# Reordering experts by size in a routed two-layer network, with the weight splits of short steps moved

## The chip, the cores and the metric

The kernel runs on one core of a Trainium2 chip. The metric is the time of one execution on the device in microseconds (us); the median of three runs of the kernel before is 1150.44 us. The trace is one profiled execution. Engines are named as in the profile: PE (TensorE, matmuls), PEld (its weight loads), DVE (VectorE), ACT (ScalarE), POOL (GpSimd) and SP (SyncE); the last two also issue transfers (DMAs).

## The reference

Three parts follow one another: a cross attention, a gated network without routing, and a network with eight experts, of which each row uses the one that wins an argmax. Only the last is touched here.

```python
def _moe2_ref(x, w_gate, w_output_gate, w1, w2):      # x: 4352 x 512
    logits = x @ w_gate
    e_idx = np.argmax(logits, axis=1)                 # one of 8 experts per row
    ...
    for e in range(E):
        mask = e_idx == e
        if not mask.any():
            continue
        h = np.maximum(x[mask] @ w1[e], 0.0)          # w1[e]: 512 x 1024
        ye = h @ w2[e]                                # w2[e]: 1024 x 512
        out[mask] = gate_w[mask, None] * eom[mask, e, None] * ye
    return out
```

With the inputs used, the reference sends 1082, 32, 576, 64, 512, 1024, 512 and 550 rows to experts 0 to 7.

## The kernel before

The first phase (attention, dense network, routing) runs to about 720 us. It writes every row into a table in device memory, sorted by expert (`ysort`), and counts the rows of each expert. The second phase is the class `Phase2`. It takes the rows expert by expert, in steps: a full step has 256 rows; what is left of an expert at its end, if it is at most 64 rows, is a step of 64 rows ("half" in the code). Which expert comes when is data: `table()` computes on DVE a rank for each expert (`rk`, by its count; the two that were largest when the first weights were fetched are forced to the front), turns it into a one-hot matrix `oh` by comparing `rk` with an iota `rr` (L1303), and from that a table with one line for each step. Each engine reads its fields into registers: `first` and `last` (this is the first, or last, step of its expert, and another expert follows), `slot`, `rank`, `half`, the experts whose weights are to be loaded (`exp2`, `exp1`) and the row to start from. Two full steps of the largest expert run ahead of that loop, with fixed addresses. What the loop then runs is, in the order before (F a full step, h one of 64 rows):

    expert  0    5     2    7    4   6   3  1
    steps   FFh  FFFF  FFh  FFh  FF  FF  h  h      steps 0 to 18

All products are done in two parts: an operand is split into a high part (ACT, a copy that rounds) and a low part (DVE, the difference), and three of the four products are summed. So the weights of each expert are loaded raw and split on ACT and DVE: w1 in four parts (`part1`, L1713 and L1769), w2 in two halves of two parts (`part2`, L1731 and L1777). There are two raw buffers for w1 (`raw1`), one raw buffer for w2 (`raw2`), one split w1 and two slots of split w2. The rules for an expert of rank r are:

- In its first step, ACT and DVE split w2 of rank r+1. When DVE has done the last part (semaphore `l21`), SP loads w2 of rank r+2 into `raw2` (L1028, one transfer of 2 MB).
- In its last step, ACT and DVE split w1 of rank r+1, each part once PE no longer needs the old one. When the last part is done (`l13`), SP loads w1 of rank r+3 (L1031, four transfers of 512 KB).

SP runs through the steps in order, and so do its transfers. An expert with one single step does both in that step.

PE's order in a full step k (L1648, L1655): `p1(k,0)`, then `p2(k-1,3)`, the last quarter of the step before (after a short step: its whole second product `n2(k-1)`), then `p1(k,1)`, `p2(k,0)`, `p1(k,2)`, `p2(k,1)`, `p1(k,3)`, `p2(k,2)`. `p1(k,j)` is a quarter of the first product (24 matmuls), `p2(k,j)` a quarter of the second (12). In a short step it is `n1(k)` (16 matmuls), `p2(k-1,3)`, and `join(k)`, which transposes and folds (16); `n2(k)` (16) follows in the next step. `p2(k,j)` waits for ACT (`hh`, L1098) and DVE (`hl`, L1104) to have split quarter j of the hidden layer; `p1(k,0)` waits for DVE's `yl(k)`, which makes the low part of the step's rows.

ACT and DVE each run a fixed list for a step (L1735 to 1759 and L1862 to 1891). They run it in order: an instruction that waits holds up all behind it. For the short step they are:

    ACT: copy 0, w1(0), copy 1, w1(1), yh(k+1), hhb 0, hhb 1, w1(2), w1(3), w2(0), w2(1)
    DVE: turn(k+1), seen 0, w1(0), seen 1, w1(1), yl(k+1), osc(k-1), hlb 0, hlb 1, w1(2), w1(3), w2(0) to w2(3)

For a full step ACT has hh(0), w2(0), w1(0), hh(1), ..., and DVE hl(0), osc(k-1), w1(0), w2(0), hl(1), turn(k+1), .... An entry w1 or w2 does something only in a last or first step. ACT's `w2(0)` (`hi2`, L1725) waits for the raw w2 to have landed (semaphore `r2`). `osc(k)` scales the finished rows of step k by their gates, in two halves of 128 rows (`gate`, L1114) or, for 64 rows, in two dependent operations (L1839, L1841); POOL then stores them and fetches the rows of step k+2. At the end, `guard.run(step, end)` calls `tail` (PE) and `osc` (DVE) for the last step, which ends with its store.

Of the kernel before, what the change touches and what calls it, by code (L numbers as in the profile page):

```python
# [14 lines left out]
ALU = mybir.AluOpType  # L15
AX = mybir.AxisListType
# [11 lines left out]
NE = 8  # L28
# [918 lines left out]
class Phase2:  # L947
# [207 lines left out]
            return self.w2[:, slot, hl, 512 * c : 512 * c + 512]  # L1155
        return self.w2[:, ds(slot, 1), hl, 512 * c : 512 * c + 512].rearrange("p a f -> p (a f)")

    def p2(self, e, k, j, slot):

        for t in range(2):  # L1160
            i = 0
            for f in range(2):
                for hh, wh in ((0, 0), (0, 1), (1, 0)):
                    m = e.matmul(  # L1164
                        out=self.ps_o[2 * (k % 2) + t],
                        lhsT=self.hT[:, j % 2, f, hh, P * t : P * t + P],
                        rhs=self.w2c(slot, wh, 2 * j + f),
                        start=j == 0 and i == 0,
                        stop=j == 3 and i == 5,
                    )  # L1170
                    i += 1
        return m

    def parts(self):
# [53 lines left out]
    def table(self, cp):  # L1228

        nc = self.nc  # L1230
        V = nc.vector
# [18 lines left out]
        e8, tie = self.e8, self.tie  # L1250
        kk = iota([1], [[0, 1]], cm=1)
        rr = iota([NE, NE], [[1, NE], [0, NE]])
        lt = t([NE, NE])
        nc.gpsimd.memset(lt, 1.0)
        nc.gpsimd.affine_select(
# [4 lines left out]
        nc.tensor.matmul(out=ps[:, 0:NE], lhsT=self.ph.ones, rhs=self.ph.cum, start=True, stop=True)  # L1260
        cnt = t([NE])
        V.tensor_copy(out=cnt, in_=ps[:, 0:NE])

        self.pad = cp.tile([P, NE + 1], I32, name="pad")
        pad = t([NE + 1])
# [34 lines left out]
        )  # L1300
        red(rk, cmp)
        oh = t([NE, NE])
        V.tensor_tensor(out=oh, in0=rk.unsqueeze(1).to_broadcast(sq), in1=rr, op=ALU.is_equal)  # L1303

        def pick(v):
# [11 lines left out]
        m = t([NE, NE])  # L1317
# [16 lines left out]
        def total(o, v, scalar, op0, u=None):  # L1334
# [53 lines left out]
            out=own,  # L1388
# [11 lines left out]

    def run(self):
        tc, nc = self.tc, self.nc
        names = "p q a d yh yl tn o os0 so r10 r11 r2".split()
        names += [f"l1{j}" for j in range(4)] + [f"h1{j}" for j in range(4)]
        names += [f"l2{p}" for p in range(2)] + [f"h2{p}{c}" for p in range(2) for c in range(2)]
        self.s = {n: tc.alloc_semaphore("m_" + n) for n in names}
        self.sy = [tc.alloc_semaphore(f"m_y{i}") for i in range(3)]
        bank = lambda n: self.ph.ps_x.tile([P, 512], F32, tag="aux", name=n)
        self.ps_t = [bank(f"ps_t{i}") for i in range(2)]

        class Guard:
            def __init__(g, eng):
                g.eng = eng
                g.total = None
                g.sure = SURE

            def __call__(g, k, body):
                if k < g.sure:
                    body()
                elif k < NSTEP:  # L1420
                    g.get()
                    with g.eng.If(g.total > k):
                        body()

            def get(g):
                if g.total is None:
                    g.total = g.eng.value_load(self.ttab[0:1, 0:1], min_val=0, max_val=NSTEP)

            def run(g, body, end):

                for i in range(SURE - 1):
                    body(i)
                g.get()

                def rest(i):
                    g.sure = i + 1
                    body(i)
                    if i + 1 == NSTEP:
                        end(i)
                        return  # L1440
                    with g.eng.If(g.total > i + 1):
                        rest(i + 1)
                    with g.eng.Else():
                        g.sure = i + 1
                        end(i)

                rest(SURE - 1)

        with tc.tile_critical(), nc.Block(no_gpsimd_drain=True) as block:
            block.sync(lambda e: self.sp(Guard(nc.sync)))  # L1450
            block.gpsimd(lambda e: self.pool(Guard(nc.gpsimd)))
            block.tensor(lambda e: self.pe(Guard(nc.tensor)))
            block.scalar(lambda e: self.act(Guard(nc.scalar)))
            block.vector(lambda e: self.dve(Guard(nc.vector)))
# [106 lines left out]
    def pe(self, guard):  # L1561
# [34 lines left out]
                after[17] = inc("p")  # L1596
            self.p1(e, j, before, after)

        def p2(k, j):
            thr = [(f"l2{j // 2}", R[k][0])] if k >= 0 else []  # L1600
            o = [("o", 2 * k)] if j == 0 else []
            wait(("d", 6 * k + j + 1 if k >= 0 else 0), *o, *thr)()
            self.p2(e, k, j, R[k][1] if k >= 0 else 0).then_inc(s["q"], 1)

        def product(out, ts, first=True, last=True):
            for i, (l, w) in enumerate(ts):
# [52 lines left out]
            tail(k - 1)  # L1659
            kinds(k, lambda: rest(k), lambda: join(k))  # L1660

        guard.run(step, tail)

    def weights(self, e, k, one, two):

# [12 lines left out]
    def act(self, guard):  # L1678
        e, s = self.nc.scalar, self.s

        def hh(k, j):
            e.wait_ge(s["p"], 5 * k + j + 1 + (j == 3))
            if k + j:
                e.wait_ge(s["q"], self.q2(k, j - 2))
            self.hhi(e, j).then_inc(s["a"], 1)

        def copy(k, n):
            e.wait_ge(s["p"], 5 * k + 2 + n)
            e.activation(out=self.hs[:, 512 * n : 512 * n + 512], in_=self.ps_h[n], func=AF.Copy).then_inc(s["a"], 1)

        def hhb(k, b):
            e.wait_ge(s["p"], 5 * k + 4 + b)
            if k + b:
                e.wait_ge(s["q"], self.q2(k, b - 2))
            e.activation(
                out=self.hTB[:, 4 * b : 4 * b + 4, 0, 0:HB],
                in_=self.ps_t[b].rearrange("p (c n) -> p c n", c=4)[:, :, 0:HB],
                func=AF.Relu,
            ).then_inc(s["a"], 1)

        def yh(k, free):

            e.wait_ge(s["tn"], k)
            for i, f in enumerate(free):
                e.wait_ge(s["p"], 5 * (k - 1) + f)
                self.yhi(e, 2 * i).then_inc(s["yh"], 1)

        def step(k):
            (kind,) = self.load(e, k, "half")

            def hi1(j, slot, rank1, rank, free):
                e.wait_ge(s["p"], 5 * k + free)
                go = lambda x: e.activation(  # L1713
                    out=self.part1(self.w1[:, 0], j), in_=self.part1(self.raw1[:, x], j), func=AF.Copy
                ).then_inc(s[f"h1{j}"], 1)
                with e.If(slot == 0):
                    if j == 0:
                        e.wait_ge(s["r10"], rank1 * 32)
                    go(0)
                with e.Else():  # L1720
                    if j == 0:
                        e.wait_ge(s["r11"], rank1 * 32 + 32)
                    go(1)

            def hi2(p, slot, rank):  # L1725
                if p == 0:
                    e.wait_ge(s["r2"], rank * 16)
                if k + p:
                    e.wait_ge(s["q"], self.q2(k - 1, 2 + p))
                for c in range(2):  # L1730
                    e.activation(  # L1731
                        out=self.w2part(slot, 0, p, c), in_=self.part2(self.raw2, p, c), func=AF.Copy
                    ).then_inc(s[f"h2{p}{c}"], 1)

            w1, w2 = self.weights(e, k, hi1, hi2)  # L1735
            with e.If(kind == 0):
                hh(k, 0)
                w2(0)
                w1(0, 1)
                hh(k, 1)  # L1740
                w2(1)
                w1(1, 2)
                hh(k, 2)
                w1(2, 3)
                guard(k + 1, lambda: yh(k + 1, (4, 5)))
                hh(k, 3)
                w1(3, 5)
            with e.Else():
                copy(k, 0)
                w1(0, 2)  # L1750
                copy(k, 1)
                w1(1, 2)
                guard(k + 1, lambda: yh(k + 1, (3, 3)))
                hhb(k, 0)
                hhb(k, 1)
                w1(2, 3)
                w1(3, 3)
                w2(0)
                w2(1)

        guard.run(step, lambda k: None)

    def dve(self, guard):
# [58 lines left out]
            with e.Else():  # L1822
                go(True)

        def osc(k):
            e.wait_ge(s["q"], self.q2(k, 3))
            if k >= 0:
                e.wait_ge(s["so"], 32 * (k + 1))

            def both():  # L1830
                if k >= 0:
                    e.sem_inc(s["os0"], 1)
                for t in range(2):
                    self.gate(e, k, t).then_inc(s["o"], 1)

            def half():
                ps = self.ps_o[2 * (k % 2)]
                o, g = self.ob[0][0:HB], self.gt[k % 4][0:HB, 0, 0:1]
                e.tensor_scalar(out=o, in0=ps[HB:P], scalar1=g, scalar2=None, op0=ALU.mult).then_inc(s["os0"], 1)  # L1839
# [19 lines left out]
        def step(k):  # L1859
# [17 lines left out]
                w2(3)  # L1877
            with e.Else():
                guard(k + 1, lambda: turn(k + 1))
                seen(k, 0)  # L1880
                w1(0)
                seen(k, 1)
# [4 lines left out]
                hlb(k, 1)  # L1887
                w1(2)
                w1(3)
                for i in range(4):  # L1890
                    w2(i)

        guard.run(step, osc)


def moe_kernel(tc, x, state, w_a, w_b, w_out, w_gate, w_og, w1, w2, out):
# [96 lines left out]
```

## Time and profile before

| | us |
|---|---|
| median of 3 runs (lowest to highest) | 1150.44 (1148.33 to 1152.05) |
| profiled execution, its own time | 1151.68 |
| its span in the trace | 1150.0 |
| PE busy in the span | 1112.3 (97%) |
| DVE busy | 625.3 (54%) |
| ACT busy | 433.9 (38%) |
| POOL busy | 293.8 (26%) |

Times in the trace count from the start of the span. A busy share is an average over stages; what a stage waits for is read from the rows of that stage. A row of a timeline gives start, length, engine, line, operation, output and inputs, the number of instructions merged, and in brackets the idle time before and what ended it.

### The profile page before, as it was taken

What the parts mean: (1) busy time and instruction counts of PE and PEld (TensorE: products, weight loads), DVE (VectorE), ACT (ScalarE), POOL (GpSimd) and SP (SyncE); (2) the same over time, 40 slices, a digit from 0 to 9 for tenths busy, and PEclk for the clock granted to TensorE, in tenths of its full rate; (3) what the DMA queues carried; (4) which work ended last, traced back from release to release, by engine and by line L of the source; (5) the groups of instructions that cost most, each with busy time, mean ns of one, the idle gap of its engine ahead of it and who ended that gap; (6) DMA issues with size and microseconds to landing.
All of it is one profiled execution on the core that took longest, in us unless ns stands there. A gap on an engine that the chain in (4) does not pass through costs nothing.

```text
span 1150.0 us, 19344 instructions
## 1 busy us (share of the span) xinstructions
PE 1112.3 (97%) x7032; PEld 892.7 (78%) x7032; DVE 625.3 (54%) x1104; ACT 433.9 (38%) x707; POOL 293.8 (26%) x394
## 2 busy tenths in 40 slices
PE   5999999999999999999999999999999999999994
PEld 3767767777777777777777799889899998889983
DVE  5877565465465555654654365763442444455553
ACT  6885333333343333333343245421421324142341
POOL 6000014032051060150330524322231232332122
PEclk9999999999999999999999999999999999999998
DMA  8662302203103013020000107638271352535520
GB/s 302 223 217 38 76 6 69 40 17 81 17 29 83 3 38 74 5 71 1 15 24 1 33 16 194 193 79 239 71 194 38 77 166 78 158 89 156 108 89 30
DMA packets 99552, 98.91 MB, mean 86 GB/s; under 512 B 60144, under 2 KB 71440, under 8 KB 99408
## 3 DMA queue, kind: packets, MB, share of 16 engines
q1 hardware_dynamic: 87976, 71.56, 22.9%
q0 software_dynamic: 11168, 25.52, 7.6%
q8 instruction: 72, 1.18, 0.4%
q14 instruction: 72, 0.59, 0.2%
q10 hardware_dynamic: 264, 0.07, 0.0%
HBM read 76.75 MB, written 21.15 MB: 85 GB/s over the span
## 4 chain that ended last, share of the span: by engine, by line
PE 87%; DVE 4%; DMA 3%; ACT 2%; issue 1%; SPq 0%; POOL 0%; DVEq 0%; POOLq 0%; ACTq 0%
PE ps_y L640 23%; PE ps_ab L621 23%; PE ps_h L1143 14%; PE ps_o L1164 13%; PE ps_m L560 4%; PE ps_sab L748 3%; PE ps_h L1607 1%; PE ps_o L1607 1%; DMA gt<-ysort 1%; DMA yT<-in_moe_w_b 1%; PE ps_l L812 1%; PE ps_sr L495 1%; PE ps_e L482 1%; PE ps_s L364 1%; DMA x<-in_x 0%
## 5 line engine op out<-in xcount | busy, mean ns | idle before, releaser
L1143 PEld LDWEIGHTS ps_h<-yT,w 128*128 128x128 f32 x1536 | 188.5, 190 | 9.2 <-issue 2.9
L1143 PE MATMUL ps_h<-yT,w 128*128 128x256 f32 x1536 | 191.6, 281 | 3.1 <-issue 2.1
L288 POOL DMA_INDIRECT ysort<-y,gdu x136 | 151.6, 1115 | 149.0 <-DVE y L921 105.5
L1164 PE MATMUL ps_o<-w,hT 128*128 (+1 forms) x768 | 187.1, 392 | 1.7 <-DVE hT L1104 1.7
L640 PE MATMUL ps_y<-gh,wo_h 128*128 128x512 f32 (+1 forms) x432 | 167.2, 391 | 2.7 <-ACT wo_h L261 2.5
L640 PE MATMUL ps_y<-gh,wo_l 128*128 128x512 f32 (+1 forms) x432 | 163.7, 382 | 0.0
L640 PE MATMUL ps_y<-gl,wo_h 128*128 128x512 f32 (+1 forms) x432 | 162.6, 380 | 0.0
L1164 PEld LDWEIGHTS ps_o<-w,hT 128*128 128x128 f32 x768 | 140.0, 188 | 29.1 <-issue 1.9
L587 DVE TENSOR_TENSOR a<-a,ps_ab 128x512 f32<-128x512 f32 x96 | 65.7, 684 | 129.1 <-PE ps_ab L621 129.0
L621 PE MATMUL ps_ab<-Ah,Mh 128*128 128x512 f32 x384 | 128.9, 415 | 0.0
L621 PE MATMUL ps_ab<-Al,Mh 128*128 128x512 f32 x384 | 120.8, 395 | 0.0
L621 PE MATMUL ps_ab<-Ah,Ml 128*128 128x512 f32 x384 | 119.6, 391 | 0.0
L1124 POOL DMA_INDIRECT out<-yT,gt x37 | 44.3, 1197 | 264.9 <-DVE yT L1114 222.9
L1098 ACT ACTIVATE hT<-ps_h 128x512 fp32r<-128x512 f32 x64 | 38.1, 595 | 194.6 <-PE ps_h L1143 187.3
L621 PEld LDWEIGHTS ps_ab<-Ah,Mh 128*128 128x128 f32 x384 | 66.5, 190 | 51.9 <-issue 41.1
L640 PEld LDWEIGHTS ps_y<-gh,wo_h 128*128 128x128 f32 x432 | 81.4, 189 | 28.7 <-issue 7.1
L591 ACT ACTIVATE gh<-a 128x512 fp32r<-128x512 f32 (+1 forms) x108 | 65.4, 605 | 99.0 <-DVE a L587 98.9
L595 DVE TENSOR_TENSOR gl<-a,gh 128x512 fp32r<-128x512 f32 (+1 forms) x108 | 71.1, 658 | 44.6 <-ACT gh L591 44.5
L583 ACT ACTIVATE a<-ps_ab 128x512 f32<-128x512 f32 x96 | 57.4, 598 | 100.2 <-PE ps_ab L621 100.2
L640 PEld LDWEIGHTS ps_y<-gl,wo_h 128*128 128x128 f32 x432 | 81.3, 189 | 16.4
L323 DVE TENSOR_TENSOR Ml<-ps_m,Mh 128x512 fp32r<-128x512 f32 x96 | 61.8, 684 | 58.7 <-ACT Mh L322 58.6
L1104 DVE SCALAR_TENSOR_TENSOR hT<-ps_h,hT 128x512 fp32r<-128x512 f32 x64 | 44.0, 688 | 89.7 <-ACT hT L1098 89.5
(269 smaller groups left out, 1395.5 us busy)
## 6 DMA issues: line engine op xcount, KB each, us to landing
raw<-in_moe_w SPq DMA_DIRECT2D x32, 512.0 KB, 10.3
raw<-in_moe_w SPq DMA_DIRECT2D x8, 2048.0 KB, 9.5
x<-in_x SPq DMA_DIRECT2D x7, 1024.0 KB
xin<-in_x SPq DMA_DIRECT2D x96, 64.0 KB
y<-ysort POOLq DMA_DIRECT2D x28, 128.0 KB, 7.2
y<-in_moe_w_a SPq DMA_DIRECT2D x6, 512.0 KB
yT<-in_moe_w_b SPq DMA_DIRECT2D x6, 512.0 KB
yT<-ysort POOLq DMA_DIRECT2D x24, 128.0 KB, 3.2
```

Of the source, the lines that this page charges most:

```text
L288: self.disjoint(self.nc.gpsimd.indirect_dma_start(**kw))
L323: self.nc.vector.tensor_tensor(out=lo, in0=src, in1=hi.bitcast(F32), op=ALU.subtract)
L560: nc.tensor.matmul(out=ps[q][32 * j : 32 * j + 32, :].rearrange("n (a f) -> n a f", a=2), lhsT=st[64 * q : 64 * q + 64, 32 * j : 32 * j + 32],
L583: nc.scalar.activation(out=d["t"][:, 0:n], in_=d["p"][0][:, 0:n], func=AF.Copy)
L587: nc.vector.tensor_tensor(out=a, in0=a, in1=d["p"][1][:, 0:n], op=ALU.mult)
L591: nc.scalar.activation(out=d["g"][0][:, 0:n], in_=d["t"][:, 0:n], func=AF.Copy)
L595: nc.vector.tensor_tensor(out=gl[:, 0:n], in0=d["t"][:, 0:n], in1=gh.bitcast(F32)[:, 0:n], op=ALU.subtract)
L621: nc.tensor.matmul(out=ps, lhsT=m[:, ab, q, c0 : c0 + P], rhs=r[:, q, :], start=i == 0, stop=i == 5)
L640: nc.tensor.matmul(out=ys[c], lhsT=l[:, f, P * c : P * c + P], rhs=r, start=f == 0 and i == 0, stop=f == NFC - 1 and i == 2,)
L1124: return e.indirect_dma_start(out=self.out, out_offset=bass.IndirectOffsetOnAxis(ap=to[0:rows].bitcast(U32), axis=0), in_=self.ob[t][0:row ...
L1143: m = e.matmul(out=self.ps_h[j % 2][:, G * (f % 2) : G * (f % 2) + G], lhsT=self.w1[:, wh, x : x + P], rhs=self.yT[:, c, yh, :], start=k == 0,
L1164: m = e.matmul(out=self.ps_o[2 * (k % 2) + t], lhsT=self.hT[:, j % 2, f, hh, P * t : P * t + P], rhs=self.w2c(slot, wh, 2 * j + f), start= ...
```

## The change

The change has four parts. In `table()`, the numbers with which `rk` is compared are shifted, if every expert has at least one row: place 2 looks for rank 7, places 3 to 5 for ranks 2 to 4, place 6 for rank 6 and place 7 for rank 5. In the step lists for 64 rows, ACT does `w2(0)` ahead of all else instead of behind w1, and DVE does `w2(0)` and `w2(1)` right behind `turn`. At the end of the kernel, a last step that is full signals a new semaphore `e` when the first 128 rows of its last quarter are summed, and DVE's gate of those rows waits for `e` rather than for the whole quarter. The wait of `osc` on PE stands, for the last step only, inside the branch instead of ahead of it.

With the row counts above the order of the loop becomes

    expert  0    5     1  2    7    4   3  6
    steps   FFh  FFFF  h  FFh  FFh  FF  h  FF      steps 0 to 18

```diff
-    def p2(self, e, k, j, slot):
+    def p2(self, e, k, j, slot, then=None):
...
                     i += 1
+            if then and t == 0:
+                then(m)
         return m
...
         rr = iota([NE, NE], [[1, NE], [0, NE]])
+        shift = t([NE, NE])
+        nc.gpsimd.memset(shift, 0.0)
+        for a, b, v in ((2, 3, 5.0), (3, 6, -1.0), (7, 8, -2.0)):
+            nc.gpsimd.memset(shift[:, a:b], v)
...
         V.tensor_copy(out=cnt, in_=ps[:, 0:NE])
+        every = t([1])
+        V.tensor_reduce(out=every.unsqueeze(2), in_=cnt.unsqueeze(1), axis=AX.X, op=ALU.min)
+        V.tensor_scalar(out=every, in0=every, scalar1=1.0, scalar2=None, op0=ALU.min)
...
         oh = t([NE, NE])
+        V.scalar_tensor_tensor(out=rr, in0=shift, scalar=every, in1=rr, op0=ALU.mult, op1=ALU.add)
         V.tensor_tensor(out=oh, in0=rk.unsqueeze(1).to_broadcast(sq), in1=rr, op=ALU.is_equal)
...
-        def p2(k, j):
+        def p2(k, j, then=None):
...
-            self.p2(e, k, j, R[k][1] if k >= 0 else 0).then_inc(s["q"], 1)
+            self.p2(e, k, j, R[k][1] if k >= 0 else 0, then).then_inc(s["q"], 1)
...
-        guard.run(step, tail)
+        guard.run(step, lambda k: kinds(k, lambda: p2(k, 3, inc("e")), lambda: n2(k)))
...
             with e.Else():
+                w2(0)
                 copy(k, 0)
                 w1(0, 2)
...
                 w1(3, 3)
-                w2(0)
                 w2(1)
...
-        def osc(k):
-            e.wait_ge(s["q"], self.q2(k, 3))
+        def osc(k, end=False):
+            if not end:
+                e.wait_ge(s["q"], self.q2(k, 3))
...
                 for t in range(2):
+                    if end:
+                        e.wait_ge(*((s["q"], self.q2(k, 3)) if t else (s["e"], 1)))
                     self.gate(e, k, t).then_inc(s["o"], 1)
...
             def half():
+                if end:
+                    e.wait_ge(s["q"], self.q2(k, 3))
...
                 guard(k + 1, lambda: turn(k + 1))
+                w2(0)
+                w2(1)
                 seen(k, 0)
...
                 w1(3)
-                for i in range(4):
-                    w2(i)
-
-        guard.run(step, osc)
+                w2(2)
+                w2(3)
+
+        guard.run(step, lambda k: osc(k, True))
```

## Rows read from the trace of the kernel before

**Rows 1.** The page: chain that ended last, share of the span by engine.
```profile
PE 87%; DVE 4%; DMA 3%; ACT 2%; issue 1%; SPq 0%; POOL 0%; DVEq 0%; POOLq 0%; ACTq 0%
```

**Rows 2.** PE's waits, 760 to 1150 us: total, times, longest.
```profile
PE ps_h L1607 <- DVE w L1769: 2.1, 1, 2.1
PE ps_h L1143 <- issue: 2.1, 1, 2.1
PE ps_o L1164 <- DVE hT L1104: 1.7, 1, 1.7
PE ps_o L1607 <- DVE hT L1797: 1.6, 1, 1.6
```

**Rows 3.** Timeline of PE, from the end of step 10 to the last product.
```profile
989.88 2.99 PE L1143 MATMUL ps_h<-yT,w 128*128 128x256 f32 x24
...
1110.74 3.83 PE L1607 MATMUL ps_h<-w,yT 128*128 128x512 f32 x16
...
1123.07 2.08 PE L1607 MATMUL ps_h<-w,yT 128*128 128x512 f32 x8 [2.13 <-DVE w L1769]
...
1132.16 5.51 PE L1607 MATMUL ps_o<-w,hT 128*128 x16 [1.60 <-DVE hT L1797]
```

**Rows 4.** Timeline of DVE and POOL at the end.
```profile
1138.27 0.75 DVE L1839 TENSOR_SCALAR yT<-ps_o,gt 64x512 f32<-64x512 f32 x1 [6.22 <-PE ps_o L1607]
1139.15 0.74 DVE L1841 SCALAR_TENSOR_TENSOR yT<-ps_o,gt,yT 64x512 f32<-64x512 f32 x1
1140.69 0.91 POOL L1124 DMA_INDIRECT out<-yT,gt  x1 [2.00 <-DVE yT L1841]
```

**Rows 5.** Timeline of PE: short step 2 (from 815.60) and full step 3.
```profile
815.60 3.82 PE L1607 MATMUL ps_h<-w,yT 128*128 128x512 f32 x16
...
823.72 3.08 PE L1143 MATMUL ps_h<-yT,w 128*128 128x256 f32 x24
...
838.60 2.91 PE L1164 MATMUL ps_o<-w,hT 128*128 x12
```

**Rows 6.** Timeline of ACT and DVE in short step 17, the first with w2 splits.
```profile
1112.93 1.25 DVE L1080 STREAM_TRANSPOSE yts<-y 128x1024 f32<-128x1024 f32 x1 [0.99 <-issue]
...
1119.53 0.74 DVE L1797 SCALAR_TENSOR_TENSOR hT<-ps_t,hT 128x256 fp32r<-128x256 f32 x2
...
1120.57 2.36 DVE L1769 TENSOR_TENSOR w<-raw,w 128x1024 fp32r<-128x1024 f32 x2 [0.30 <-ACT w L1713]
...
1122.84 4.62 DVE L1777 TENSOR_TENSOR w<-raw,w 128x1024 f32 x4
```

**Rows 7.** Timeline of ACT and DVE around the start of step 3.
```profile
822.31 1.29 DVE L1095 TENSOR_TENSOR yT<-yts,yT 128x512 fp32r<-128x512 f32 x2
...
829.25 2.00 ACT L1731 ACTIVATE w<-raw 128x1024 f32 x2
...
829.46 0.69 DVE L1104 SCALAR_TENSOR_TENSOR hT<-ps_h,hT 128x512 fp32r<-128x512 f32 x1 [1.42 <-ACT hT L1098]
```

**Rows 8.** Timeline: DVE's last w2 part in step 10, SP's next load.
```profile
990.83 1.23 DVE L1777 TENSOR_TENSOR w<-raw,w 128x1024 f32 x1 [1.01 <-DVEq L1786]
...
992.22 0.40 SPq L1028 DMA_DIRECT2D raw<-in_moe_w  x1
```

**Rows 9.** Line L1028, the six loads of w2 in the loop.
```profile
DMA to landing us min/median/max: 8.7/9.5/26.8
```

**Rows 10.** Transfers issued from 969 to 973 us: KB each, median us to landing.
```profile
y<-ysort POOLq DMA_DIRECT2D x4, 128.0 KB, 10.1
```

**Rows 11.** Timeline of PE at the loop's entry, after 2.1 us idle.
```profile
769.90 4.62 PE L1143 MATMUL ps_h<-yT,w 128*128 128x256 f32 x24 [2.10 <-issue]
...
777.15 2.90 PE L1143 MATMUL ps_h<-yT,w 128*128 128x256 f32 x24
```

**Rows 12.** The stretch behind that entry: PE busy, granted clock, DMA share, GB/s.
```profile
770.00:775.00 5.00, 5.00 (x27) 0.66 0.89 185
```

**Rows 13.** Timeline of DVE in the table's computation.
```profile
739.83 0.23 DVE L1303 TENSOR_TENSOR srT<-srT 128x64 f32<-128x64 f32 x1
```

More of the change, by code (lines that the diff above doesn't have):

```diff
@@ L1402, in run @@
         tc, nc = self.tc, self.nc
-        names = "p q a d yh yl tn o os0 so r10 r11 r2".split()
+        names = "p q e a d yh yl tn o os0 so r10 r11 r2".split()
         names += [f"l1{j}" for j in range(4)] + [f"h1{j}" for j in range(4)]
```

## Prediction

> **What bounds the kernel now.** I read the chain that ended last first: PE holds 87% of it [rows 1], so only what makes PE wait, what slows PE, or what stands behind its last matmul can change the time. PE's waits in the second phase come next [rows 2]: four, 7.5 us together. The 2.1 us ended by "issue" is the entry into the loop, which the change does not touch. The 1.7 us (split hidden layer, L1104) falls in step 10, a full step behind a short one. The other two are in the last two steps: 2.13 us for w1's low part, 1.60 us for the short hidden layer [rows 3]. There two experts of one short step each follow each other, and each of those steps has to split 4 MB of weights on ACT and DVE beside three groups of 16 matmuls. The last product also shows a slower PE: 16 matmuls of 512 columns took 5.51 us where 16 such at 1110.74 took 3.83 [rows 3].
>
> So about 5.4 us are to be had at the end, if the new order shows no wait of its own. The sum of PE's work is the same, the steps being only permuted; I therefore add up idle and slow time before and after.
>
> **What goes.** Waits of 2.13 and 1.60, and 5.51 - 3.83 = 1.7 us of slow clock: the new end is two full steps with nothing left to load or split. Tail: PE ends at 1132.16 + 5.51 = 1137.67, the first gate starts at 1138.27, and the last store at 1140.69, 3.0 us behind PE [rows 4]. In the new end the gate of the first 128 rows is under the second half of the last quarter, and behind PE stand the start of DVE (0.16, an estimate from the step from DVE's end at 992.06 to SP's issue at 992.22 [rows 8]), one gate of 0.75 and the 0.8 us that POOL takes from the second operation's end at 1139.89 to the store [rows 4]: 1.7 us, so 1.3 us less. But the last store carries 128 rows and another 128-row store goes out just ahead of it; no row prices that at this place. Bounds 0 to 1.3, I take 0.6. Gone in all: 2.1 + 1.6 + 1.7 + 0.6 = 6.0 us.
>
> **What comes: the small expert in third place.** Step 7 is now short and alone in its expert. It splits w2 of rank 3, and only when DVE has finished (`l21`) may SP load w2 of rank 4 into the one raw buffer. Step 8 is full and the first of rank 3, and has to split just that w2. Before, a load had a whole full step or more between; only experts of one step lack it, and those stood where nothing was left to load. How late is it? I count from the start of the short step.
>
> DVE first. In short step 17 of the trace `turn` starts at 1112.93 - 1110.74 = 2.2 and ends at 3.4 [rows 3, 6]. Behind it now stand: two w2 parts (2.3, half of the 4.62 for four), two w1 parts (2.4), `yl` for a full step (1.3), the two gates (1.5, from 0.75 for one of 512 columns), two `hlb` (0.75), two w1 parts (2.4), two w2 parts (2.3) [rows 4, 6, 7]. That is 13.0, so `l21` comes at 16.4, an estimate from these durations laid end to end; ACT's list is shorter and runs ahead. SP issues the load 0.2 us later [rows 8], and it lands in 9.5 [rows 9]: at 26.1. ACT stands in step 8 at `w2(0)`, behind `hh(0)`, and behind it wait `hh(1)` and through it DVE's `hl(1)`: 2.0 for the two copies [rows 7], about 0.6 for `hh`, 0.7 for `hl` [rows 7], and some 0.3 for starts. `p2(8,1)` can run at 29.7.
>
> PE second. In steps 2 and 3 the same matmul group, L1164 at 838.60, starts 23.0 us behind the short step's start [rows 5]. In step 7 `yl` is late, because two w2 parts are put ahead of it: it has its first half at 3.4 + 2.3 + 2.4 + 0.65 = 8.8, its start on PE at 9.0, where PE is free at 823.72 - 815.60 = 8.1 [rows 5]. So PE waits 0.9 us there, and reaches `p2(8,1)` at 23.9.
>
> The gap is 29.7 - 23.9 = 5.8 us. Its bounds are 4.5 (landing in 8.7, `turn` earlier by 0.4) and 7.5 (`l21` and landing each a microsecond later). The trace then shows what idle PE pays at its restart: behind the 2.1 us at the entry, 24 matmuls took 4.62 us against 2.90 later [rows 11], with a mean granted clock of 0.66 in that stretch, that is, part of it at 1.2 GHz rather than 2.4 [rows 12]. I add 1.7 us. The bound below is 0, since the 2.13 us wait in step 17 was followed by eight matmuls of normal length, 2.08 us [rows 3]; a gap of 5.8 is nearer to the case that paid, being longer than any gap in the rows.
>
> **The short step in place 6** (step 16): two small splits stand ahead of `yl` here too, so 0.9 us as above (bounds 0 to 1.5). There is no load behind it. Its follower's `p2(17,0)` has about 1 us of slack against DVE's list; the bound above takes that in. Moving ACT's `w2(0)` to the front costs nothing: it runs under PE's first eight matmuls, whose result `copy 0` waits for anyway; if that cover were gone it would delay `copy 0` by 2.0 us, and the fold has 3.6 us before it needs it. DVE's move is the one that costs, and is priced above.
>
> **Small things.** A full step behind a short one has a first quarter of 3.08 us against 2.90 [rows 5, 11]; there are five such pairs instead of three: 0.3 us. The table gets three more DVE operations, at most 0.23 each [rows 13]; they stand in a chain that PE waits for only briefly: bounds 0 and 0.7, I take 0.3. The memsets are on POOL, ahead of the counts, with POOL idle: 0 (if it were busy they would be late for the comparison only if by several microseconds). The moved wait of `osc`, and the signal on a matmul, add no work. The 1.7 us wait behind step 9 stays: the short steps of the experts with 576 and 550 rows come one place later, as steps 10 and 13, with the same followers and loads. Bounds -1.7 and +1.7.
>
> **Sum.** Comes: 0.9 + 5.8 + 1.7 + 0.9 + 0.3 + 0.3 = 9.9. Goes: 6.0. Net +3.9 us. The profiled execution took 1151.68 (its span is 1150.0), 1.2 above the median; +3.9 gives 1155.6 for it and **1154.3 us** for the median of 1150.44.
>
> **Rivals.**
>
> *The new gap is short* (a chance of 0.15). If the load is hidden but for 2 us and the clock holds, the sum is 0.9 + 2.0 + 0.9 + 0.6 - 6.0 = -1.6: 1148.8 us. For: the list of DVE has waits in it that might overlap better than end to end. Against: 16.4 would have to be 12.6.
>
> *The load is out of ACT's way* (0.08), the case on the other side. If `l21` came at 10.6 or earlier, the raw w2 would be there when PE needs the split, and the gap and its slow clock would vanish: 2.4 - 6.0 = -3.6, 1146.8 us, faster. It decides from the moment that DVE has 5.8 us less ahead of `l21`. Only the splits, 9.4 us of them, are large enough, and all four w2 parts have to be done by then; the rows show no such slack.
>
> *The load shares the engines* (0.17). POOL fetches the rows of step 9 just ahead of that load, and in the trace such a fetch of four times 128 KB beside a weight load landed in 10.1 us [rows 10]: both suffer. The fetch is a quarter of the load's bytes, so the load could take a quarter longer, 2.4 us, and the gap with it. PE's steady pace is a second item of this case: 24 matmuls took 2.90 at 777 and 2.99 at 990 [rows 11, 3], and if the slower pace follows on a gap, it would begin some two full steps earlier, 8 quarters of 0.1: 0.8. Sum 3.9 + 2.4 + 0.8 = 7.1: 1157.5 us. The Trainium skill ("DMA: Bandwidth & Descriptors", section "Queues, rings and completion order") says that each DMA engine goes round the queues that have work for it, packet by packet. By that rule a fetch that is still under way delays the load by up to its own bytes, and no run here shows yet which of the two pays.
>
> *As forecast* (0.60): +1.5 to +6.5 by the bounds, 1152 to 1157.
>
> **Chances and range.** A measurement of this kernel can tell about 0.3% from no change, 3.45 us. In the likeliest case +3.9 lies just beyond; I give it 0.6 of its chance slower and 0.4 the same, 0.36 and 0.24. With the shared engines (0.17 slower), the short gap (0.15 same, 0.02 of that faster) and the hidden load (0.08 faster): slower 0.53, same 0.37, faster 0.10. The range of 8 in 10 runs from the short gap's 1148.8, a little lower, to the shared engines' 1157.5 and a little above: 1148 to 1159; the hidden load and some of the worst cases are left out.
>
> **What would show it.** In the new trace the waits at the end (2.1 and 1.6) are gone and PE's last group is at the clock of the groups before. Near 937 us, in the full step behind the short one at 913, PE waits some 5.8 us for DVE's L1104, with ACT's L1731 idle before it until the load of L1028 lands; the granted clock is low right behind. PE waits about 0.9 us for `yl` behind both short steps. SP's issue of that load stands some 16.6 us behind the short step's start. I am wrong if that wait is under 3 us, if a wait elsewhere takes its place, if the clock does not fall behind it, or if the end behind PE's last matmul shrinks by more than 2 us.

## The result, and the profile after

The changed kernel is slower: 1162.23 us (median of 6 runs, 1160.45 to 1165.27) against 1151.24 for the kernel before in the same comparison (6 runs, 1148.33 to 1156.69). The ratio is 1.0099, 95% interval 1.0078 to 1.012: 11 us more, where 3.9 were forecast, and above the range.

PE's waits from 760 us on, in the profile after (total, times, longest), answer to [rows 2]:

```profile
PE ps_t L1646 <- issue: 5.0, 1, 5.0
PE ps_o L1164 <- DVE hT L1104: 4.9, 2, 4.4
PE ps_h L1143 <- issue: 2.1, 1, 2.1
PE ps_o L1164 <- issue: 0.4, 1, 0.4
```

Both waits at the end are gone, as forecast. The gap in step 8 is there, 4.4 us. The largest wait is new: 5.0 us ahead of the fold (`join`, ps_t), ended by "issue", that is, by nothing that the profile can name. PE's timeline shows where it stands, in short step 7, which begins at 916.15:

```profile
916.15 3.83 PE L1617 MATMUL ps_h<-w,yT 128*128 128x512 f32 x16
919.81 2.92 PE L1164 MATMUL ps_o<-w,hT 128*128 x12
927.72 3.68 PE L1646 MATMUL ps_t<-tri,srT 128*128 128x64 f32 x16 [5.00 <-issue]
931.16 5.28 PE L1143 MATMUL ps_h<-yT,w 128*128 128x256 f32 x24
...
945.50 2.91 PE L1143 MATMUL ps_h<-yT,w 128*128 128x256 f32 x24
952.83 4.60 PE L1164 MATMUL ps_o<-w,hT 128*128 x12 [4.42 <-DVE hT L1104]
...
1146.98 3.06 PE L1164 MATMUL ps_o<-w,hT 128*128 x12 [0.37 <-issue]
```

The data of the fold was there: ACT's two copies ended by 920.6. Behind either gap PE is slow; behind the one in step 8 the granted clock is 0.50 from 954 to 956. For the one in step 7, the stretches (PE busy, granted clock, DMA share, GB/s) show the lower level, 1.2 GHz, and DMA engines that are full:

```profile
923.00:925.00 2.00, 0.00 (x0) 1.00 1.05 219
925.00:927.00 2.00, 0.00 (x0) 0.71 0.99 190
927.00:929.00 2.00, 1.28 (x6) 0.50 0.98 221
929.00:931.00 2.00, 2.00 (x12) 0.50 0.62 184
```

What fills them is step 6's load of w1, which SP issues one microsecond into step 7. The timeline of SP and ACT, and behind it the issue of the w2 load (KB, median us to its landing), answer to [rows 8, 9]:

```profile
917.19 1.82 SPq L1031 DMA_DIRECT2D raw<-in_moe_w  x4
...
937.72 0.40 SPq L1028 DMA_DIRECT2D raw<-in_moe_w  x1
...
949.48 2.00 ACT L1741 ACTIVATE w<-raw 128x1024 f32 x2 [10.47 <-DMA raw<-in_moe_w]
```
```profile
raw<-in_moe_w SPq DMA_DIRECT2D x1, 2048.0 KB, 11.6
```

The end is the second surprise. Its chain in order of time (start, length, what), answering to [rows 4]:

```profile
1146.06 0.06 DVEq L1451
1146.12 4.11 issue
1150.22 0.30 DVEq L1200
...
1150.79 0.10 DVE yT L1114
...
1153.62 0.98 POOL out L1124
```

DVE takes its last branch (L1451) at 1146.06 and loads its next register, in the code of the end, 4.1 us later. PE's last matmul ends at 1146.98 + 3.06 = 1150.04. So the gate of the first 128 rows, which was to run under the last half quarter, comes behind it, and the last store starts 3.6 us behind PE, not 1.7.

The spans differ by 13.6 us. Of these, 2.1 lie ahead of the loop's entry (771.97 against 769.90 [rows 11]). Of the kernels run below on chips of about the same speed, four with the new table enter at 770.1, 770.3, 770.8 and 772.5 and two with the old one at 771.1 and 771.4, so the entry scatters whatever the table, and I do not count the 2.1 us to the change. From the entry on it is 11.5 us: the late fold 5.2 (927.72 against 919.81 + 2.75), the slow fold 1.7 and the slow quarter behind it 2.2, the gap in step 8 4.6, its slow quarter 1.7, less 5.4 for the old end and 1.2 for the wait behind step 9, which is now 0.48 us behind step 13, plus 0.4 for PE's own jump at the end and 1.2 for the longer tail (13.6 us behind PE instead of 12.3). That is 10.4. Of the 1.1 us left, some 0.4 is PE's steady pace: 24 matmuls take 2.99 us instead of 2.91 in 23 pairs of quarters here, in 19 before. The rest I did not follow.

### The profile page after: what moved, and what is told of

Read it like the earlier page. It is cut to its first block, busy times and chain, and to the rows that moved or that the text cites. A ratio compares the mean times of both kernels' runs of the same rounds, so it can differ in the third digit from the quotient of the medians.

```text
span 1163.6 us, 19345 instructions
## 1 busy us (share of the span) xinstructions
PE 1117.8 (96%) x7032; PEld 897.2 (77%) x7032; DVE 625.1 (54%) x1107; ACT 434.0 (37%) x707; POOL 293.5 (25%) x398
## 5 line engine op out<-in xcount | busy, mean ns | idle before, releaser
L1143 PEld LDWEIGHTS ps_h<-yT,w 128*128 128x128 f32 x1536 | 191.0, 192 | 9.1 <-issue 2.9
L1143 PE MATMUL ps_h<-yT,w 128*128 128x256 f32 x1536 | 194.3, 283 | 3.1 <-issue 2.1
L640 PEld LDWEIGHTS ps_y<-gl,wo_h 128*128 128x128 f32 x432 | 81.4, 189 | 16.4
```

Source lines behind the costliest of these rows:

```text
L640: nc.tensor.matmul(out=ys[c], lhsT=l[:, f, P * c : P * c + P], rhs=r, start=f == 0 and i == 0, stop=f == NFC - 1 and i == 2,)
L1143: m = e.matmul(out=self.ps_h[j % 2][:, G * (f % 2) : G * (f % 2) + G], lhsT=self.w1[:, wh, x : x + P], rhs=self.yT[:, c, yh, :], start=k == 0,
```

## The experiments

Theory A: PE's wait in step 7 is for its own code, that is, for instructions. It jumps there over the list of a full step, the block with the target has to be fetched by a transfer, and that transfer stands among the packets of the w1 load. Rivals: the place in the code costs this wherever the load is (B); ACT's w2 copies at the front of the step hold up the fold (C). Four of the ten runs (named below) were on another chip, on which the kernel before takes 1187.25 us; the others were on two chips with 1153.43 and 1152.16 us. Ratios are to the kernel before on the same chip.

**The load taken out of step 7.** SP issues step 6's w1 load behind step 7's w2 load:

```diff
+            if k == 7:
+                ones(*(self.load(e, 6, *FIELDS[:7])[i] for i in (1, 2, 3, 6)))
+            if k != 6:
+                ones(last, slot, rank1, exp1)
...
+        def ones(last, slot, rank1, exp1):
             with e.If(last > 0):
```

> The changed kernel, with one load moved: the w1 load that SP issues in step 6, and that runs through short step 7, is issued behind step 7's w2 load. Theory A (PE jumps in step 7 to code that has to be fetched, and the fetch stands behind that load on the DMA engines): PE's 5.0 us ahead of the fold (ps_t) vanish, and with them the slow clock of the fold and of the first quarter behind it, 1.7 and 2.2 us: some 9 us less, about 1153 us. The gap of 4.4 us before the second quarter of step 8 stays, or grows by 1 to 2 us, as PE comes to it earlier. Theory B (the jump to that place in the code costs 5 us whatever the DMA engines do): no change, about 1162 us. Theory C (the fold waits for ACT, held up by its w2 copies at the front of the step): no change either, about 1162 us.

1160.12 us, ratio 1.0062 (1.0044 to 1.0081). The wait at the fold and its slow clock are gone; the gap in step 8 has grown to 9.3 us. PE's timeline, step 7 beginning at 911.57, and the landing of the w2 load:

```profile
917.99 1.90 PE L1652 MATMUL ps_t<-tri,srT 128*128 128x64 f32 x16
...
920.02 3.00 PE L1143 MATMUL ps_h<-yT,w 128*128 128x256 f32 x24
...
944.37 4.38 PE L1164 MATMUL ps_o<-w,hT 128*128 x12 [9.27 <-DVE hT L1104]
```
```profile
raw<-in_moe_w SPq DMA_DIRECT2D x1, 2048.0 KB, 13.7
```

B falls: same code, no wait. The gain is half of what was expected, because 4.8 of the 9 us came back in step 8: PE is there earlier, and the w2 load takes 13.7 us.

The transfers of one microsecond each show the code block itself (queue of instructions: packets, MB, share). In the changed kernel it comes between 924 and 925, in this run between 914 and 915:

```profile
q8 instruction: 1, 0.02, 8.6%
```
```profile
q8 instruction: 1, 0.02, 8.8%
```

In steps of 0.1 us, the blocks stand at 924.8 and 914.9. That is 8.7 us into step 7 under the load, and 3.4 without it: 5.3 us later, for a wait of 5.0. The profile doesn't name the engine that a block is for; that this one is PE's is read from the times, gathered in the table further down.

**The order alone,** with the old lists and the old end:

> The kernel before with the new order of experts alone: step lists and end as before. Theory A: PE's wait ahead of the fold of step 7 is as in the changed kernel, 5 us with a slow clock behind it, and so is the gap in step 8, as the load of w2 comes at about the same time: 1160 to 1164 us. Theory C (the w2 copies at the front of the short step cause the wait ahead of the fold): that wait is gone, about 1153 us.

1166.9 us, ratio 1.0105 (1.0079 to 1.0131): more than the 1160 to 1164 us expected, but the interval overlaps with that of the changed kernel. PE's waits:

```profile
PE ps_o L1164 <- DVE hT L1104: 5.4, 2, 4.8
PE ps_t L1644 <- issue: 4.8, 1, 4.8
```

C falls: the lists are the old ones, and the wait is there. The whole loss is the order's; the new lists and the gated end give nothing that can be measured.

**The lists alone,** with all shifts zero (other chip):

```diff
-        for a, b, v in ((2, 3, 5.0), (3, 6, -1.0), (7, 8, -2.0)):
+        for a, b, v in ((2, 3, 0.0), (3, 6, 0.0), (7, 8, 0.0)):
```

> The changed kernel with the old order of experts (all shifts zero); the step lists and the gate at the end stay changed. Theory A (the lists matter only for a short step that is its expert's only one, here 17, and there two w2 parts ahead of w1 make w1 late): PE's wait for w1 near 1121 us grows from 2.1 to about 4.5 us, no wait as in step 7, 1152 to 1154 us. Theory C (the lists alone cost the 11 us): 1162 us.

Ratio 1.0011 (0.9988 to 1.0034): no change, and C falls here too. But the wait for w1 did not grow, it is 2.2 us:

```profile
PE ps_h L1617 <- DVE w L1779: 2.2, 1, 2.2
```

So w1's last parts are not late because of DVE's list, as I had it; they wait for ACT, whose list ahead of them is as long as before.

**A load put into another short step.** If A holds, the kernel before must show the wait too when a load runs through one of its short steps. First a copy within device memory:

```diff
+            if k == 2:
+                e.wait_ge(s["q"], 8)
+                src = self.w[0][0].rearrange("(c a j) f -> a j c f", a=4, j=32)
+                dst = self.spare.rearrange("p (c f) -> p c f", c=4)
+                for a in range(4):
+                    e.dma_start(out=dst[32 * a : 32 * a + 32], in_=src[a]).then_inc(s["x"], 16)
...
```

> The kernel before, old order, with a transfer added that no result needs: when short step 2 begins, SP copies 2 MB of one expert's w1 within device memory, in four pieces as a weight load. Theory A (the code fetch stands behind transfers): PE, which goes through step 2 without a wait, now waits 4 to 6 us ahead of the fold, ended by nothing that the profile shows, and then runs slow: 6 to 10 us more, about 1158 to 1161 us. Theory B (place in the code): PE passes step 2 as before; at most 1 us more from later row fetches, 1151 to 1152 us.

1151.43 us, ratio 0.9985 (0.9965 to 1.0005), no wait in step 2. A miss, but a weak test: the copy's pieces landed in 5.9 us each and the DMA share lay at 0.6 to 1.0 for some 6 us, where the weight load held 1.0 for 10. The second block of step 2 came at 821.5, 6.4 us into the step instead of 3.8, and still 4.6 us ahead of its use. So, on the other chip, the real load, into the buffer that already holds the same data:

```diff
+            if k == 2:
+                e.wait_ge(s["r10"], 64)
+                ex = e.value_load(self.ttab[0:1, 2:3], min_val=0, max_val=NE - 1)
+                e.wait_ge(s["q"], 8)
+                get(0, ex, self.raw1[:, 0], "x")
...
```

> The kernel before, old order, with one transfer added that changes no data: when short step 2 begins, SP loads the raw w1 of the third expert (2 MB, four pieces) once more into the buffer that already holds it, so the same kind of load as the one that runs through step 7 of the changed kernel, in place of a copy within device memory, which was over sooner and did not fill the DMA engines. Theory A (the code that PE jumps to is fetched behind such a load): PE waits 4 to 6 us ahead of the fold of step 2 (at about 822 us), where it did not wait, and the fold and the quarter behind it are slow: 6 to 10 us more than before. Theory B (it is the place in the code, or the order): no wait there, within 1.5 us of before.

Ratio 1.0016 (1.0001 to 1.0032). This is a miss as well: A had the wait at the fold, with 4 to 6 us. The fold ran on time; a wait of 1.3 us came one product later. PE's timeline, step 2 beginning at 852.27:

```profile
858.68 1.89 PE L1641 MATMUL ps_t<-tri,srT 128*128 128x64 f32 x16
860.38 2.98 PE L1143 MATMUL ps_h<-yT,w 128*128 128x256 f32 x24
864.70 3.98 PE L1612 MATMUL ps_o<-w,hT 128*128 x16 [1.33 <-issue]
```

By the code's packets it can be read why. In the kernel before, step 2 gets blocks between 814 and 815 and between 819 and 820, that is 1.6 to 0.6 us ahead of its start at 815.60 and 3.4 to 4.4 us behind it. The row of the second, and behind it that of the second block here, between 861 and 862:

```profile
q8 instruction: 1, 0.02, 6.0%
```
```profile
q8 instruction: 1, 0.02, 8.6%
```

Here the first came before the load had begun, and the second 8.7 to 9.7 us behind the start: 5 us late, as in step 7, but with more time to its use. Issued some 5 us earlier (`q` at 7 instead of 8, on the chip with 1152.16 us), the load should catch the first block:

> The kernel before, old order, with the same needless load of a raw w1 as in the run that put it at the start of step 2, issued some 5 us earlier, in the last quarters of step 1. There the load held up PE's second block of code, and the wait came at the second product of step 2 (1.3 us) and not ahead of the fold; the first block had come about 1 us ahead of the step. Theory A: now the first block is requested under the load, comes 4 to 6 us late, and PE waits 1 to 5 us in step 2 itself, ahead of its first product, the last quarter of step 1 or the fold, ended by nothing that the profile shows. Theory B (place in the code): no such wait in step 2.

1154.5 us, ratio 1.0026 (1.0003 to 1.0048). The first block came between 819 and 820, 3.5 to 4.5 us behind the step's start at 815.52 and thus 5 us late again; PE waited ahead of the fold, though only 0.6 us where 1 to 5 were expected:

```profile
822.65 2.00 PE L1641 MATMUL ps_t<-tri,srT 128*128 128x64 f32 x16 [0.57 <-issue]
```

The table has the blocks and the group of PE that follows on each, read in steps of 0.1 us. "Load" says whether one runs when the block comes, "behind the block" how long after it PE's group starts, and "idle ahead" how long PE had waited then (all in us).

| kernel, step, block | load | block, from the step's start | PE's group starts | behind the block | idle ahead |
|---|---|---|---|---|---|
| changed, 7 | yes | 924.8, 8.7 | fold 927.72 | 2.9 | 5.0 |
| order alone, 7 | yes | 926.0, 8.5 | fold 928.94 | 2.9 | 4.8 |
| load moved, 7 | no | 914.9, 3.4 | fold 917.99 | 3.0 | 0 |
| load behind the fold (next run), 7 | no | 917.6, 3.4 | fold 920.67 | 3.0 | 0 |
| before, 2, first | no | 814.4, -1.2 | fold 822.01 | 7.6 | 0 |
| early load, 2, first | yes | 819.7, 4.2 | fold 822.65 | 2.9 | 0.6 |
| before, 2, second | no | 819.3, 3.8 | second product 826.63 | 7.3 | 0 |
| load in step 2, second | yes | 861.5, 9.3 | second product 864.70 | 3.2 | 1.3 |

So such a load delays a block by 5.1 to 5.5 us in all four cases, and wherever PE waited, it went on 2.9 to 3.2 us behind the block. What PE pays is the delay less the time that it had to spare: some 4.5 us in step 2, and almost none in step 7, where the undisturbed block came 3.0 us ahead of the fold. No run moves the code itself.

**The load behind the fold.** In the changed kernel SP waits with step 6's w1 load until the fold's first half is done:

```diff
+            if k == 6:
+                e.wait_ge(s["p"], 39)
             with e.If(last > 0):
```

> The changed kernel; step 6's w1 load still runs in step 7 and ahead of the w2 load, but SP issues it only when PE has done the first half of the fold of step 7, some 6 us later. Theory A (only what PE has to fetch while the load runs comes late): no wait ahead of the fold, which starts some 6.4 us behind the step's start; the code is there before the load begins. The gap in step 8 is 4 to 9 us, as the two loads share what is left of step 7. Theory B (a load in step 7 costs PE this wait wherever it stands): a wait of about 5 us somewhere in step 7 or the first quarters of step 8.

1162.78 us, ratio 1.008 (1.0061 to 1.0099). The fold starts 6.4 us into the step without a wait, as A says. The gap in step 8 is 12.4 us, above the 4 to 9 that I had expected, as w2's load now runs behind the whole w1 load. PE's timeline:

```profile
920.67 1.89 PE L1648 MATMUL ps_t<-tri,srT 128*128 128x64 f32 x16
...
950.15 5.37 PE L1164 MATMUL ps_o<-w,hT 128*128 x12 [12.37 <-DVE hT L1104]
```

**The gap in step 8.** To the moved load is added a later place for step 8's w2 parts:

```diff
                 hh(k, 0)
-                w2(0)
+                if not late:          # late = k == 8
+                    w2(0)
                 w1(0, 1)
                 hh(k, 1)
-                w2(1)
+                w2(0 if late else 1)
                 w1(1, 2)
                 hh(k, 2)
+                if late:
+                    w2(1)
```

and on DVE `w2(0)` stands behind `hl(k, 1)`, `turn` and `w1(1)` there.

> As the run with the moved w1 load, and in step 8 alone ACT and DVE do the first w2 parts one place later in their lists (ACT behind hh 1 instead of hh 0, its second half behind hh 2; DVE behind hl 1). Theory A for the gap (ACT stands at w2 until the raw weights land, and hh 1 stands behind it): the wait before the second quarter of step 8 goes, and the slow clock behind it: 4.4 + 1.7 us less than that run, about 1147 us, with at most 1 to 2 us left before the third quarter. Theory B (POOL's fetch and stores hold DVE up there): the wait stays, 1153 us.

1153.17 us, ratio 0.9999 (0.9984 to 1.0013), so 0.6% or 7 us less than with the moved load alone, where 6.1 less were expected. (The expected 1147 us supposed 1153 for the run with the moved load, which took 1160.) The 9.3 us are now two waits of 2.8 and 1.55. The first has another cause, DVE's timeline shows it: DVE stands at `osc` of step 7 until the stores of step 6 have landed:

```profile
935.92 0.75 DVE L1864 TENSOR_SCALAR yT<-ps_o,gt 64x512 f32<-64x512 f32 x1 [7.85 <-DMA out<-yT,gt]
```

Theory A for the gap holds for most of it, and its rival for the 2.8 us. Ahead of the 1.55 ACT and DVE still do w2: ACT's copy starts at 941.32, when the load has landed.

**DVE's branch at the end,** taken ahead of `hl(k, 3)` (other chip). The rest of the full step's list becomes `close`, which stands in both arms of the branch:

```diff
                     with g.eng.If(g.total > i + 1):
+                        close(i)
                         rest(i + 1)
                     with g.eng.Else():
                         g.sure = i + 1
+                        close(i)
                         end(i)
...
+        def close(k):
+            kind, w1, w2 = K[k]
+            with e.If(kind == 0):
+                hl(k, 3)
+                w1(3)
+                w2(3)
```

> The changed kernel with the moved w1 load and the later w2 parts of step 8, and DVE's branch to the code of the end taken ahead of the last hl 3 instead of behind it. Theory A (DVE's 4.1 us ended by nothing that the profile shows, between its last branch and the load of its register, are the fetch of the code at the end): the branch now runs under DVE's wait of 4.9 us for ACT, the first gate starts before PE's last matmul ends, and the last store starts 1.7 us behind PE instead of 3.6: about 2 us less than with those two moves alone, 1151 us where that was 1153. Theory B (DVE waits there for a semaphore): the first gate stays behind PE's end, 1153 us.

Ratio 1.0 (0.9983 to 1.0018). The trace shows what was expected; PE, DVE and POOL at the end:

```profile
1170.97 3.01 PE L1164 MATMUL ps_o<-w,hT 128*128 x12 [0.48 <-issue]
1172.64 0.75 DVE L1114 TENSOR_SCALAR yT<-ps_o,gt 128x512 f32<-128x512 f32 x1 [3.54 <-PE ps_o L1164]
...
1175.57 0.97 POOL L1124 DMA_INDIRECT out<-yT,gt  x1 [0.40 <-issue]
```

The first gate now waits for PE alone, and the last store starts 1.6 us behind PE's end at 1173.98. The kernel without this branch started it 3.0 us behind (1139.50 against 1136.52). The 1.4 us are in the trace; in the time they are within the interval.

**All w2 parts of step 8 at its end,** and `osc` of step 7 behind `hl 1`, on top of that (other chip):

> The run before, and in step 8 ACT and DVE do all w2 parts at the end of their lists, and DVE does osc of step 7 behind hl 1. If what is left of PE's waits in step 8 (2.8 and 1.6 us) comes from DVE standing at osc until the stores have landed, and from ACT and DVE standing at w2 until the load has landed, both go: 4 us less than the run before, about 1147 us, faster than the kernel before by some 0.4%. If the late load only moves the wait to the first quarter of step 9, 1149 to 1151 us.

Ratio 0.9958 (0.9941 to 0.9974), 1182.72 against 1187.25 us. Nothing is left of the wait in step 8, and PE's waits for the hidden layer in the whole loop are

```profile
PE ps_o L1164 <- DVE hT L1104: 0.3, 1, 0.3
```

By its ratio this kernel is faster than both, with the new order.

## Why the prediction was wrong

- **The end.** Right: the waits of 2.1 and 1.6 us and the slow last product are gone.
- **The step that failed** is the second paragraph: "The sum of PE's work is the same, the steps being only permuted; I therefore add up idle and slow time before and after." The list of idle times held only waits for data. PE also waits for its own instructions, and the new order puts a weight load into a short step, where PE jumps. The prediction names step 6's w1 load nowhere and thus puts its effect at nothing. In step 7 it costs 5.2 us at the fold and 3.9 of slow clock, 9.1 together. Not all of it is lost: without the load PE comes to step 8 earlier and waits there 4.8 us longer, so taking the load out gives back 4.3 us (1.0099 against 1.0062). Of the 7.1 us between forecast and result, about 4.3 are thus the load's, and about 3.5 the gap in step 8, which was forecast at 5.8 and is 9.3 without the late fold; these are estimates from one run each, and add up to a little more. That the load is the cause of the wait at the fold is shown by taking it out, in two ways (wait gone), and by putting such a load into step 2 (a wait appears, of 0.6 or 1.3 us). That it acts by the code block is read from the table: the block comes 5.1 to 5.5 us later under the load, and PE goes on some 3 us behind it. The Trainium skill ("Runtime: NRT & Kernel Launch", section "Instruction fetch mechanics") says that a jump to code outside of what the sequencer holds forces a transfer of the block before it can go on. These traces agree, with blocks of 0.02 MB on the instruction queue; I had not weighed that rule.
- **The gap in step 8.** Mechanism right, 5.8 us forecast, 4.6 measured, and that this is near is partly luck. It is the difference of two sizes that were both off: w2's last part came 21.4 us into the step, not 16.4 (in the run with the moved load 15.5), because DVE's `hlb` stood behind the late fold, and the load took 11.6, not 9.5; PE was 8 us late itself. (By their own terms the bounds add up to 4.6 and 7.8, not 4.5 and 7.5.) The rival "the load shares the engines" was real in the run with the moved load, and too small: there the w2 load took 13.7 us, 4.2 more than forecast, not 2.4. (That "both suffer" is not in its rows: beside the fetch of 10.1 us the w1 load landed in 9.1, below its median of 10.3 on the page.) The rival counted the 0.5 MB of the fetch; POOL's queue moved 0.79 MB beside the load (927 to 942), stores among them, and by the rival's own rate that is 3.6 us, an estimate. The Trainium skill's rule of engines going round the queues ("DMA: Bandwidth & Descriptors", section "Queues, rings and completion order") agrees, and the load pays: from 932 to 937 both queues moved packets in each microsecond, and SP's fell from some 0.3 MB in each to between 0.11 and 0.24. In the changed kernel itself POOL's fetch was over (0.03 MB from 937 to 950); SP issues step 7's own w1 load 1.0 us behind the w2 load (938.72 against 937.72), but whether that made it 11.6 is not shown. The rival's second item, a slower steady pace behind a gap, did not come: with the clock back behind either gap 24 matmuls took 2.89 to 2.91 us, and 2.99 from 849 on, where no gap stood.
- **Slow clock behind the gap.** Forecast 1.7, measured 4.43 - 2.75 = 1.7. The mechanism is right, the size in part luck: the entry [rows 11], from which it was taken, took 4.6 us in seven of the twelve kernels and 3.0 to 3.1 in the other five, behind the same 2.1 us of idle PE. Behind the waits of 2.8 and 1.55 us in the run with later w2 parts no quarter was slow (3.0 us); behind each gap in step 8 from 4.4 us on one was (4.4 to 5.4).
- **The waits for `yl`.** Forecast 0.9 twice; 0.3 in step 7 when the fold is on time (920.02 against 917.99 + 1.70), 0 in step 16. `yl`'s first half ended about 8.4 and 7.9 us into these steps, not 8.8.
- **The tail.** Wrong in direction: forecast 0.6 us less, measured 1.2 more. The new gate stands behind a branch of DVE that takes 4.1 us; before, that branch ran under the wait for PE [rows 4]. Taking the branch earlier gives the early gate in the trace, so the branch was the cause.
- **Small things.** The table cost nothing visible, by the entries above; the wait behind a short step shrank from 1.7 to 0.5 us, within its bounds.

## What to carry to other kernels

In a kernel with branches, an engine's own code can be one more transfer, as it was for PE here: before work is moved, look at which jumps the engine takes while the DMA engines are full, and place large loads away from them or jump earlier, under a wait that is there anyway. A wait named "issue" at a branch, beside a full DMA share, is the sign. When a reorder shortens the time between a buffer's release and its next use, add what else uses the DMA engines then, and move the consumer in each engine's list rather than let it hold up what stands behind it.

## What the runs showed that I had not expected

A block of 0.02 MB of instructions came 5.1 to 5.5 us later when a 2 MB weight load was under way, in four cases. A branch to code far ahead cost DVE 4.1 us with DMA engines all but idle (share 0.05 from 1146 to 1150). POOL's second store of a step took 4.5 us instead of 1.0 in step 7 of the run with the moved load (and in step 16 of the changed kernel), and it is part of why the stores landed late there. In these two and three more cases DVE runs w1 and w2 splits back to back meanwhile, and the store ends 0.87 to 0.89 us behind the last of them; in step 7 of the changed kernel, where no split runs beside it, it took 1.00. So the splits seem to hold it, but no run takes them away.
